# A gated attention and MLP kernel: four kinds of product share five PSUM banks in place of three and two

## The chip, the cores and the metric

The kernel runs on one core of one Trainium2 chip. The metric is device time in microseconds of one execution: the median of three runs before the change is 814.69 us (810.98 to 815.75).

## What is computed

The input x holds 2048 tokens of 512 numbers. Two branches read it: causal attention with 32 heads of 16 numbers and a sliding window of 256 tokens, and a two-layer MLP with 1792 hidden units and the tanh form of GELU. A gate, one number for each token, mixes them.

```python
def _A_ref(x, wqkv, wo):
    ...
    scores = jnp.einsum("bhqd,bhkd->bhqk", q, k) * (Dh ** -0.5)
    mask = (idx[:, None] - idx[None, :] >= 0) & (idx[:, None] - idx[None, :] < W)
    scores = jnp.where(mask[None, None], scores, -1e9)
    p = _softmax(scores, axis=-1)
    o = jnp.einsum("bhqk,bhkd->bhqd", p, v)
    return (lambda x, *d: x.transpose(*d))(o, 0, 2, 1, 3).reshape(B, S, D) @ wo

def _B_ref(x, w1, b1, w2, b2):
    h = _gelu(jnp.einsum("bsd,df->bsf", x, w1) + b1)
    return jnp.einsum("bsf,fd->bsd", h, w2) + b2

g = _sigmoid((x * gate_w).sum(-1, keepdims=True))
return g * a + (1 - g) * b
```

## The kernel before

The dense matrix products (the projections qk and v, the MLP's two layers u and y, the output projection a) are each made of three matmuls, since every operand is split into a high and a low part (`mm3`, lines 100 to 103). They work on tiles of 128 rows by 512 columns.

Attention takes four heads at a time: eight groups of heads, and in each 16 blocks of 128 tokens, so 128 steps of four heads. In each step and for each head three things happen.

- `att_max` (line 380) multiplies a block of 128 queries with up to 384 keys. This is the *maxima product*, the tile sm. VectorE adds a mask to it and takes each query's largest score (line 394, tile jm, the result in M).
- `att_exp` (line 424) multiplies a block of 128 keys with up to 384 queries, so that keys lie along the partitions. This is the *exponentials' product*, the tile st. ScalarE takes its exponential into pt (line 445), and GpSimd then zeroes what lies outside the window (lines 437 and 440).
- `att_pv` (line 451) multiplies those weights with the values (tile pv, line 465); ScalarE copies the finished sum out (line 476).

The maxima run six blocks ahead of the exponentials (LEAD). After each two blocks `att_rows` (line 400) negates the maxima on VectorE, and `att_turn` (line 409) turns them by a matmul with the identity: the *turned product*, tile mp. ScalarE writes it into 16 rows of the queries (line 418), so that the subtraction of the maximum is part of the exponentials' product. At the start of the kernel `qkv_x` (line 196) transposes blocks of x through TensorE: the *transposed product*, tile xp, which ScalarE and VectorE read.

The order of the instructions on TensorE, VectorE, ScalarE and GpSimd is written out by hand. The loop from line 708 issues for each head a maxima product, an exponentials' product, at one place the weighted sums and the turned product, and then as much dense work as the step's share of time (`fill`, 'mspf' in ORDER). Work of the other engines that follows from a product is put on a list with a due time by `after`, and `tick` advances a clock of planned times and issues what is due. Those planned times don't depend on PSUM. SP, which issues the DMAs, is left to a scheduler that orders by its own estimate of time. Each engine carries out its instructions in the order of its queue.

PSUM has eight banks, and each tile here takes one. Tiles with the same tag share as many banks as `bufs` says. A product whose bank still holds an unread one waits on TensorE, and all that follows it there waits too. Before, the banks were divided in this way: two for dense products (tag d), three for sm, mp and xp (tag sm), two for st (tag st), one for pv. Which of the banks of its tag a tile gets is settled when the program is built, from the same estimate of time that orders SP.

Of the kernel before, what the change touches and what calls it, by code (L numbers as in the profile page):

```python
# [9 lines left out]
F32 = mybir.dt.float32  # L10
# [11 lines left out]
NC = D // 128  # L22
# [10 lines left out]
def gated_mix(ctx: ExitStack, tc: tile.TileContext, x, wqkv, wo, w1, b1, w2, b2, gate_w, out):  # L33
# [7 lines left out]
    ps = ctx.enter_context(tc.tile_pool(name="ps", bufs=1, space=PSUM))  # L41
# [3 lines left out]
    def f32(ap):  # L45
        return ap.bitcast(F32)
# [61 lines left out]
    def after(ns, fn, *args):  # L108
        now[1] += 1
        heapq.heappush(todo, (now[0] + ns, now[1], fn, args))  # L110
# [7 lines left out]
    def tick(ns):  # L118
        now[0] += ns
        while todo and todo[0][0] <= now[0]:  # L120
            step_todo()

    def need(*keys):
        for key in keys:
            while key not in done:
                step_todo()
# [69 lines left out]
    def qkv_x(t, b):  # L196

        if b == 0:
            if t < NT - 1:
                v = (ks[:, 0], ks[:, 1], qs)[t].rearrange("p a c -> p (a c)")  # L200
                v = v.rearrange("p (c s t) -> p c s t", c=NC, s=2)
            else:
                v = sb.tile([128, NC, 2, T], F32R, tag="xt", bufs=1, name=f"xt{t}")
            xts[t] = v
        xt = xts[t]
        xr = xrs[t, b]
        p = ps.tile([128, NC, 128], F32, tag="sm", bufs=3, name=f"xp{t}_{b}")
        for c in range(NC):
            nc.tensor.transpose(p[:, c], xr[:, c * 128:(c + 1) * 128], ident)
        tick(4 * 110)  # L210

        def hi():
            nc.scalar.activation(xt[:, :, 0, b * 128:(b + 1) * 128], p, AF.Copy)

        def lo():
            nc.vector.tensor_sub(xt[:, :, 1, b * 128:(b + 1) * 128], p,
                                 f32(xt[:, :, 0, b * 128:(b + 1) * 128]))
            done.add(("x", t, b))
        after(100, hi), after(500, lo)
# [66 lines left out]
    def qkv(t):  # L286
# [4 lines left out]
        if t == 0:  # L291
            keys = qk + [("v", c) for c in range(NC)]
            load_xr(0)
            for key in keys[0:4]:
                load_raw(key, True)
            warm(WARM[0])
            for b in range(NB):
                qkv_x(0, b)
            warm(WARM[1])
            split(keys[0], nc.vector)  # L300
            split(keys[1], nc.vector)
            nc.sync.dma_start(gwb, gate_w.partition_broadcast(128))
        need(*[("x", t, b) for b in range(NB)])
        for n, (kind, j) in enumerate(pieces):
# [38 lines left out]
            if not last and n in xat:  # L343
                qkv_x(t + 1, xat.index(n))
# [35 lines left out]
    def att_max(g_, b, i):  # L380

        if b % RB == 0 and (g_, b // RB) not in Ms:
            Ms[g_, b // RB] = sb.tile([128, RB, 4], F32, tag="M", bufs=2, name=f"M{g_}_{b}")
        M = Ms[g_, b // RB]
        k0 = max(b - 2, 0) * 128
        w = (b + 1) * 128 - k0
        pr, s = divmod(i, 2)
        p = ps.tile([128, 384], F32, tag="sm", bufs=3, name=f"sm{g_}_{b}_{i}")
        nc.tensor.matmul(p[:, :w], qs[0:96, pr, b * 128:(b + 1) * 128], ks[0:96, pr, s, k0:k0 + w],  # L389
                         start=True, stop=True)  # L390
        junk = sb.tile([128, 384], BF16, tag="jm", bufs=1, name=f"jm{g_}_{b}_{i}")

        def red():
            nc.vector.tensor_tensor_reduce(junk[:, :w], p[:, :w], mask[:, 384 - w:384], 1.0, -3e38,  # L394
                                           ALU.add, ALU.max, M[:, b % RB, i:i + 1])
            done.add(("max", g_, b, i))
        tick(w / 2.4 + 13)
        after(100, red)
# [10 lines left out]
    def att_turn(g_, rb):  # L409

        need(("nm", g_, rb))
        p = ps.tile([112, 128], F32, tag="sm", bufs=3, name=f"mp{g_}_{rb}")
        nc.tensor.matmul(p, nms[rb % 2], identr, start=True, stop=True)  # L413

        def put():
            for b in range(RB):
                cols = slice((rb * RB + b) * 128, (rb * RB + b + 1) * 128)
                nc.scalar.activation(qs[96:112, :, cols], p[96:112].unsqueeze(1).broadcast_to([16, 2, 128]),  # L418
                    AF.Copy, scale=odd[96:112, b:b + 1])
            done.add(("rows", g_, rb))  # L420
        tick(67)
        after(100, put)

    def att_exp(g_, kb, i):

        pr, s = divmod(i, 2)
        w = min(384, S - kb * 128)
        if s == 0:
            pts[g_, kb, pr] = sb.tile([128, 2, 384], F32, tag="pt", bufs=11, name=f"pt{g_}_{kb}_{pr}")
        pt = pts[g_, kb, pr]  # L430
        need(*[("rows", g_, b) for b in range(kb // RB, (kb + w // 128 - 1) // RB + 1)])
        p = ps.tile([128, 384], F32, tag="st", bufs=2, name=f"st{g_}_{kb}_{i}")
        nc.tensor.matmul(p[:, :w], ks[:, pr, s, kb * 128:(kb + 1) * 128],  # L433
                         qs[:, pr, kb * 128:kb * 128 + w], start=True, stop=True)

        def sel():
            nc.gpsimd.affine_select(out=pt[:, :, 0:128], in_=pt[:, :, 0:128], pattern=[[0, 2], [1, 128]],  # L437
                                    compare_op=ALU.is_ge, fill=0.0, base=0, channel_multiplier=-1)
            if w == 384:
                nc.gpsimd.affine_select(out=pt[:, :, 256:384], in_=pt[:, :, 256:384], pattern=[[0, 2], [-1, 128]],  # L440
                                        compare_op=ALU.is_ge, fill=0.0, base=-1, channel_multiplier=1)
            done.add(("pt", g_, kb, pr))

        def exp():
            nc.scalar.activation(pt[:, s, :w], p[:, :w], AF.Exp, scale=SCALE)  # L445
            if s == 1:
                after(500, sel)
        tick(w / 2.4 + 13)
        after(100, exp)
# [258 lines left out]
    for u in range(-LEAD, NU):  # L708
        m = u + LEAD
        gm, bm = divmod(m, NKB)  # L710
        step = STEP if u >= 0 else STEP0
        for i in range(4):
            for op in ORDER:
                if op == "s" and u >= 0:
                    att_exp(u // NKB, u % NKB, i)
                if op == "m" and m < NU:
                    att_max(gm, bm, i ^ XOR)
                if op == "p" and i == PVAT and u >= 1:
                    att_pvs(u - 1)
                if op == "p" and i == PVAT and turn:  # L720
                    att_turn(*turn)
                    turn = None
                if op == "f":
                    fill(step / 4 / ORDER.count("f"))
        if m < NU and bm % RB == RB - 1:
            after(900, att_rows, gm, bm // RB)
            turn = (gm, bm // RB)
        if m % NB == LPOS and chunks:
            att_load(*chunks.pop(0))
        if u % NB == 2 and -NB < u < NU - NB:  # L730
            att_load_v(*divmod(u // NB + 1, NT))
# [47 lines left out]
```

## Time and profile before

| | |
|---|---|
| median of three runs | 814.69 us |
| the profiled execution, its own time | 813.36 us |
| span from its first to its last instruction | 811.4 us |
| stretch with attention steps of both kinds | about 157 to 760 us |
| granted TensorE clock | 1.000 |

The profile is of one execution. PE is TensorE's matmuls and PEld its weight loads, DVE is VectorE, ACT ScalarE, POOL GpSimd and SP the engine that issues DMAs; a trailing q (SPq) is the sequencer of an engine. A group's row gives the line, the engine, the operation, output<-input with shapes and the count; behind the first bar the busy time in us and the mean of one in ns; behind the second the idle time of the engine directly before these instructions, and what ended most of it. A row of the timeline gives start and duration in us, engine, line and operation, the count of merged instructions, and in brackets the idle time before it with what ended it. A row of a list of waits gives the sum in us, how many there were, and, where there is a third number, the longest. A view of one line lists what ended the idle time of its engine: us, then times.

### The profile page before, as it was taken

To read this page: it belongs to the slowest core of one execution; us is meant where nothing else is said; L and a number is where in the kernel's file an instruction comes from. 1 tells how busy PE (TensorE), PEld (TensorE's weight loads), DVE (VectorE), ACT (ScalarE), POOL (GpSimd) and SP (SyncE) were. 2 spreads that over 40 slices of the span, in tenths; PEclk is the share of its full clock that TensorE was granted. 3 is DMA by queue.
4 is the path that set the end of the run, shared out by engine and by line. 5 is a ranking of instruction groups with operands and counts; after the bars stand their busy time and mean duration, and the time that the engine had idled before them with its cause. 6 is when DMAs were issued, how large, how long until landed. Compare 5 with 4: busy or idle time off the path is not lost.

```text
span 811.4 us, 14841 instructions
## 1 busy us (share of the span) xinstructions
PE 788.5 (97%) x4694; PEld 616.6 (76%) x4694; DVE 513.7 (63%) x1517; ACT 483.4 (60%) x993; POOL 338.7 (42%) x611
## 2 busy tenths in 40 slices
PE   8999999999999999999999999999999999999998
PEld 6788888867877777688767867877777778777767
DVE  5433332887478758856885688568757865784353
ACT  4434423587568557755875677567656764876631
POOL 3200002396336425542784386336524552574100
PEclk9999999999999999999999999999999999999999
DMA  8985856536542734443234555542664363335873
GB/s 260 387 308 195 304 174 211 195 89 215 164 137 66 227 116 119 122 156 104 86 101 132 171 156 173 152 143 86 192 179 129 99 202 113 97 118 186 249 260 117
DMA packets 94925, 135.72 MB, mean 167 GB/s; under 512 B 32256, under 2 KB 43776, under 8 KB 94848
## 3 DMA queue, kind: packets, MB, share of 16 engines
q1 hardware_dynamic: 94848, 134.79, 52.3%
q8 instruction: 37, 0.61, 0.3%
q14 instruction: 40, 0.33, 0.1%
HBM read 79.70 MB, written 55.05 MB: 166 GB/s over the span
## 4 chain that ended last, share of the span: by engine, by line
PE 78%; DVE 8%; ACT 7%; DMA 2%; issue 2%; SPq 1%; POOL 1%; POOLq 0%; DVEq 0%; ACTq 0%
PE st L433 9%; PE pv L465 9%; PE sm L389 8%; PE y L101 6%; PE y L103 6%; PE y L102 6%; PE u L101 4%; PE u L102 4%; PE u L103 4%; PE qk L101 3%; PE qk L103 3%; PE qk L102 3%; DVE jm L394 2%; ACT pt L445 2%; PE v L103 2%
## 5 line engine op out<-in xcount | busy, mean ns | idle before, releaser
L394 DVE CUSTOM_DVE_ANT_0 jm<-sm,mask 128x384 bf16<-128x384 f32 (+2 forms) x512 | 270.6, 528 | 150.1 <-PE sm L389 128.7
L445 ACT ACTIVATE pt<-st 128x384 f32<-128x384 f32 (+2 forms) x512 | 231.0, 471 | 120.6 <-PE st L433 102.9
L437 POOL TENSOR_SCALAR_AFFINE_SELECT pt<-pt 128x256 f32<-128x256 f32 x256 | 122.3, 478 | 248.8 <-ACT pt L445 248.2
L433 PE MATMUL st<-qs,ks 128*128 128x384 f32 (+2 forms) x512 | 172.1, 338 | 8.1 <-ACT pt L445 7.1
L389 PE MATMUL sm<-ks,qs 96*128 96x384 f32 (+2 forms) x512 | 169.6, 332 | 1.8 <-DVE M L394 0.8
L433 PEld LDWEIGHTS st<-qs,ks 128*128 128x128 f32 x512 | 97.0, 190 | 37.1 <-ACT pt L445 19.4
L389 PEld LDWEIGHTS sm<-ks,qs 96*128 96x128 f32 x512 | 96.2, 188 | 26.0 <-DVE M L394 5.2
L440 POOL TENSOR_SCALAR_AFFINE_SELECT pt<-pt 128x256 f32<-128x256 f32 x224 | 101.9, 455 | 0.0
L465 PE MATMUL pv<-pt,vbuf 128*32 128x384 f32 (+2 forms) x1408 | 91.6, 389 | 0.1
L101 PE MATMUL y<-w,h 128*128 128x512 f32 x224 | 89.4, 399 | 0.0
L103 PE MATMUL y<-w,h 128*128 128x512 f32 x224 | 87.7, 391 | 1.3 <-POOL h L574 1.3
L102 PE MATMUL y<-w,h 128*128 128x512 f32 x224 | 87.7, 391 | 0.0
L574 POOL TENSOR_TENSOR h<-x1h,h 128x512 fp32r<-128x512 f32 x56 | 72.5, 1294 | 35.6 <-DVE h L571 35.2
L101 PE MATMUL u<-mx,w 128*128 128x512 f32 x196 | 79.3, 404 | 0.0
L102 PE MATMUL u<-mx,w 128*128 128x512 f32 x196 | 76.7, 391 | 0.0
L103 PE MATMUL u<-mx,w 128*128 128x512 f32 x196 | 76.6, 391 | 0.0
L418 ACT ACTIVATE qs<-mp,odd 16x256 fp32r<-16x256 f32 x128 | 53.0, 460 | 38.9 <-PE mp L413 37.9
L465 PEld LDWEIGHTS pv<-pt,vbuf 128*32 128x32 f32 x1408 | 38.5, 109 | 37.2 <-issue 24.2
L562 DVE SCALAR_TENSOR_TENSOR sqh<-sqh,x1h 128x512 f32<-128x512 f32 x56 | 51.6, 921 | 13.2 <-ACT sqh L559 13.2
L565 ACT ACTIVATE sqh<-sqh 128x512 f32<-128x512 f32 x56 | 35.5, 634 | 36.8 <-DVE sqh L562 36.2
L160 POOL TENSOR_TENSOR w<-raw_w,w 128x512 fp32r<-128x512 f32 x28 | 38.4, 1370 | 40.3 <-ACT w L156 40.2
L256 DVE TENSOR_TENSOR qke<-qk,qke 128x512 fp32r<-128x512 f32 x32 | 22.1, 691 | 51.3 <-ACT qke L253 49.6
(122 smaller groups left out, 1247.7 us busy)
## 6 DMA issues: line engine op xcount, KB each, us to landing
mx<-XT SPq DMA_DIRECT2D x24, 512.0 KB
SQ<-qke SPq DMA_DIRECT2D x16, 512.0 KB
SK<-qke SPq DMA_DIRECT2D x16, 512.0 KB
qs<-SQ SPq DMA_DIRECT2D x64, 128.0 KB
ND<-nd SPq DMA_DIRECT2D x32, 256.0 KB
ks<-SK SPq DMA_DIRECT2D x60, 128.0 KB
raw_w<-in_B_w_dram SPq DMA_DIRECT2D x28, 256.0 KB
SV<-vx SPq DMA_DIRECT2D x16, 272.0 KB
```

Source lines behind the costliest of these rows:

```text
L101: nc.tensor.matmul(p, lh, rh, start=first, stop=False)
L102: nc.tensor.matmul(p, lh, rl, start=False, stop=False)
L103: nc.tensor.matmul(p, ll, rh, start=False, stop=last)
L389: nc.tensor.matmul(p[:, :w], qs[0:96, pr, b * 128:(b + 1) * 128], ks[0:96, pr, s, k0:k0 + w], start=True, stop=True)
L394: nc.vector.tensor_tensor_reduce(junk[:, :w], p[:, :w], mask[:, 384 - w:384], 1.0, -3e38, ALU.add, ALU.max, M[:, b % RB, i:i + 1])
L418: nc.scalar.activation(qs[96:112, :, cols], p[96:112].unsqueeze(1).broadcast_to([16, 2, 128]), AF.Copy, scale=odd[96:112, b:b + 1])
L433: nc.tensor.matmul(p[:, :w], ks[:, pr, s, kb * 128:(kb + 1) * 128], qs[:, pr, kb * 128:kb * 128 + w], start=True, stop=True)
L437: nc.gpsimd.affine_select(out=pt[:, :, 0:128], in_=pt[:, :, 0:128], pattern=[[0, 2], [1, 128]], compare_op=ALU.is_ge, fill=0.0, base=0, ch ...
L440: nc.gpsimd.affine_select(out=pt[:, :, 256:384], in_=pt[:, :, 256:384], pattern=[[0, 2], [-1, 128]], compare_op=ALU.is_ge, fill=0.0, base= ...
L445: nc.scalar.activation(pt[:, s, :w], p[:, :w], AF.Exp, scale=SCALE)
L465: nc.tensor.matmul(pv[32 * i:32 * i + 32, q - c * T:e - c * T], vt[:, 68 * (kb % NB) + 17 * i:68 * (kb % NB) + 17 * i + 32], pts[g_, kb, i ...
L574: nc.gpsimd.tensor_sub(h[:, 1], x1, f32(h[:, 0]))
```

## The change

The four tags of attention's and the transposes' products become one tag with five banks. The instructions and their order in the source stay; the count of banks stays eight.

```diff
 def qkv_x(t, b):
-        p = ps.tile([128, NC, 128], F32, tag="sm", bufs=3, name=f"xp{t}_{b}")
+        p = ps.tile([128, NC, 128], F32, tag="s", bufs=5, name=f"xp{t}_{b}")
 ...
 def att_max(g_, b, i):
-        p = ps.tile([128, 384], F32, tag="sm", bufs=3, name=f"sm{g_}_{b}_{i}")
+        p = ps.tile([128, 384], F32, tag="s", bufs=5, name=f"sm{g_}_{b}_{i}")
 ...
 def att_turn(g_, rb):
-        p = ps.tile([112, 128], F32, tag="sm", bufs=3, name=f"mp{g_}_{rb}")
+        p = ps.tile([112, 128], F32, tag="s", bufs=5, name=f"mp{g_}_{rb}")
 ...
 def att_exp(g_, kb, i):
-        p = ps.tile([128, 384], F32, tag="st", bufs=2, name=f"st{g_}_{kb}_{i}")
+        p = ps.tile([128, 384], F32, tag="s", bufs=5, name=f"st{g_}_{kb}_{i}")
```

## The prediction

> **What bounds the kernel now.** The page comes first: its busy shares, its chain and its costliest groups.
>
> ```profile
> span 811.4 us, 14841 instructions
> ...
> PE 788.5 (97%) x4694; PEld 616.6 (76%) x4694; DVE 513.7 (63%) x1517; ACT 483.4 (60%) x993; POOL 338.7 (42%) x611
> ...
> PE 78%; DVE 8%; ACT 7%; DMA 2%; issue 2%; SPq 1%; POOL 1%; POOLq 0%; DVEq 0%; ACTq 0%
> ...
> L394 DVE CUSTOM_DVE_ANT_0 jm<-sm,mask 128x384 bf16<-128x384 f32 (+2 forms) x512 | 270.6, 528 | 150.1 <-PE sm L389 128.7
> L445 ACT ACTIVATE pt<-st 128x384 f32<-128x384 f32 (+2 forms) x512 | 231.0, 471 | 120.6 <-PE st L433 102.9
> ```
>
> TensorE is the bound: 97% busy, 78% of the chain. The engines that empty the four kinds of product are free a third of the time: VectorE waits 128.7 us for maxima products (sm) and ScalarE 102.9 us for exponential products (st). So this change can win only what TensorE loses to a bank that is not yet empty. The views of the lines L433 and L389 tell what ended TensorE's idle time before them (matmuls and weight loads added together), and here are their complete lists, with the one that counts stand-alone waits:
>
> ```profile
>   ACT pt L445: 26.5, 54
> ...
>   DVE M L394: 6.0, 16
>   ACT qs L418: 3.5, 7
> ...
> L389 PEldq EVENT_SEMAPHORE  x165: 51/51/51, 129.4 to 732.5; - x165
> ```
>
> No DMA is in these lists. Together 36.0 us, but a stalled product shows its gap twice, under its matmul and under its weight load. What it truly costs is read from start to start, in the timeline:
>
> ```profile
> 161.78 0.44 PE L389 MATMUL sm<-ks,qs 96*128 96x384 f32 x1 [0.44 <-DVE M L394]
> ...
> 398.89 0.55 DVE L394 CUSTOM_DVE_ANT_0 jm<-sm,mask 128x384 bf16<-128x384 f32 x1
> ...
> 399.29 0.33 PE L433 MATMUL st<-qs,ks 128*128 128x384 f32 x1
> ...
> 399.59 0.56 DVE L394 CUSTOM_DVE_ANT_0 jm<-sm,mask 128x384 bf16<-128x384 f32 x1
> ...
> 399.79 0.34 PE L433 MATMUL st<-qs,ks 128*128 128x384 f32 x1
> ...
> 400.30 0.56 DVE L394 CUSTOM_DVE_ANT_0 jm<-sm,mask 128x384 bf16<-128x384 f32 x1
> ...
> 400.65 0.34 PE L389 MATMUL sm<-ks,qs 96*128 96x384 f32 x1
> ...
> 400.92 0.87 ACT L445 ACTIVATE pt<-st 128x384 f32<-128x384 f32 x2
> ...
> 401.46 0.19 PEld L433 LDWEIGHTS st<-qs,ks 128*128 128x128 f32 x1 [0.85 <-ACT pt L445]
> 401.46 0.44 PE L433 MATMUL st<-qs,ks 128*128 128x384 f32 x1 [0.48 <-ACT pt L445]
> ...
> 402.44 0.34 PE L389 MATMUL sm<-ks,qs 96*128 96x384 f32 x1
> ...
> 402.61 0.34 PE L433 MATMUL st<-qs,ks 128*128 128x384 f32 x1
> ...
> 403.47 0.34 PE L389 MATMUL sm<-ks,qs 96*128 96x384 f32 x1
> ...
> 403.94 0.19 PEld L433 LDWEIGHTS st<-qs,ks 128*128 128x128 f32 x1 [0.51 <-ACT pt L445]
> ...
> 404.42 0.49 ACT L445 ACTIVATE pt<-st 128x384 f32<-128x384 f32 x1 [0.15 <-PE st L433]
> ...
> 717.99 0.44 PE L433 MATMUL st<-qs,ks 128*128 128x384 f32 x1 [0.40 <-ACT pt L445]
> ```
>
> Unhindered, st starts 0.17 us after its sm (402.44, 402.61). At 401.46 it started 0.81 us after it, so 0.64 us are lost, where the view shows 0.48 + 0.85. At 403.94 it lost 0.47 - 0.17 = 0.30 us, where it shows 0.51. Per microsecond shown that is 0.94 / 1.84 = 0.51, and 36.0 x 0.51 = 18.4 us. Taking the same difference for every sm, st and turned (mp) product that started within 0.12 us of the emptying of its bank, I find 48 waits, from one before the sm at 161.78 to one before the st at 717.99, and 17.4 us in all: 13.5 at 33 st, 3.9 at 15 sm, none at mp. **17.4 us is all that banks cost now**, 2.1% of the time.
>
> **The change, part by part.**
>
> *Order.* Within TensorE, VectorE, ScalarE and GpSimd no instruction moves; counts and durations stay. Moved are waits, which follow from what the bank of a product held before, and some DMA issues on SP. The built program fixes the bank of each product. It doesn't count the five banks round, but hands out whichever bank its planner thinks free first. For the 48 waits of today it gives:
>
> ```
> bank's last product: before -> after          waits   us now   us left
> st: st two back      -> an sm                   22      9.1      2.2
> st: st two back      -> an mp or older st        3      1.9      0
> st: st two back      -> the same st              8      2.5      2.5
> sm: sm               -> an st or older sm        5      1.3      0
> sm: sm or mp         -> one emptied as late     11      2.6      2.5
> ```
>
> "Left" is the same subtraction again, with the end of the emptying that the changed bank waits for, everything else at its time of today. Example: the st at 401.46 gets the bank of the sm whose maxima ran from 400.30 to 400.86, so nothing holds it at 400.65 + 0.17. **Relieved: 17.4 - 7.2 = 10.2 us.**
>
> *New waits.* By the same subtraction 17 products that start freely today find their new bank still full: 4.9 us in all. Five (1.2 us) are st behind late maxima or a late turned product: the st of 399.29 gets a bank whose maxima ran from 398.89 to 399.44, and the st at 399.79 one whose maxima end at 400.15, so TensorE gives up 0.36 + 0.05 = 0.41 us by there. In seven (1.7 us) an sm gets the bank of the st *directly before it*; in five (2.0 us) the product two before. The dearest:
>
> ```profile
> 613.49 0.34 PE L433 MATMUL st<-qs,ks 128*128 128x384 f32 x1
> ...
> 613.67 0.34 PE L389 MATMUL sm<-ks,qs 96*128 96x384 f32 x1
> ...
> 613.93 0.88 ACT L445 ACTIVATE pt<-st 128x384 f32<-128x384 f32 x2 [0.88 <-PE st L433]
> ```
>
> One exponential of this shape takes 0.49 us (404.42), so the first of the pair that starts at 613.93 ends at 614.42. From an emptying to its waiter it is 0.05 us (the pair of 400.92: 401.41, and st at 401.46). So the sm of 613.67 starts at 614.47, 0.80 us later. Behind it in TensorE's queue stand the next st, three dense matmuls and the weighted sums (pv); VectorE and ScalarE wait for those.
>
> *What the rest costs.* TensorE gets 39 more stand-alone waits: 39 x 51 ns = 2.0 us at worst; I take 0, since the 165 of today's sm products end none of the idle time in their list. The turned products wait behind other banks in 27 of 64 cases, but follow the weighted sums, which cover it; I take 0, at worst 0.8 us each. The transposes of x go from three banks to five; they wait for DMA alone:
>
> ```profile
> L209 PE MATMUL xp<-identr,xr 128*128 128x128 f32 x64 | 9.9, 280 | 2.4 <-DMA xr<-in_A_x_dram 2.4
> ...
> SPq L477 <- ACT nd L476: 96.8, 29, 9.9
> ...
> 206.66 0.30 SPq L354 DMA_DIRECT2D qs<-SQ  x1
> ...
> 223.43 0.34 PE L389 MATMUL sm<-ks,qs 96*128 96x384 f32 x1
> ```
>
> On SP, stores of weighted sums (L477) move past loads of keys (L353, L354) by a few places, a load of wo by a dozen. Such a store holds the queue up to 9.9 us. The loads behind it have a lead: one of the shortest runs from 206.66 to the first sm that needs its chunk at 223.43, 16.8 us, and no DMA ends a wait of L389. I take 0; without that cover one late chunk would cost up to 9.9 us.
>
> *Sum at rest:* -10.2 + 4.9 = -5.3 us. But an emptying that is late because its engine is busy doesn't come earlier when TensorE does. The cluster above, worked through: 0.94 relieved, 0.41 new, so TensorE is 0.5 us ahead at 403.94. Then:
>
> ```profile
> 406.72 1.33 DVE L562 SCALAR_TENSOR_TENSOR sqh<-sqh,x1h 128x512 f32<-128x512 f32 x1
> ...
> 407.97 0.55 DVE L394 CUSTOM_DVE_ANT_0 jm<-sm,mask 128x384 bf16<-128x384 f32 x1
> ...
> 408.58 0.19 PEld L389 LDWEIGHTS sm<-ks,qs 96*128 96x128 f32 x1 [0.31 <-DVE M L394]
> ...
> 409.54 0.44 PE L433 MATMUL st<-qs,ks 128*128 128x384 f32 x1 [0.52 <-ACT pt L445]
> ```
>
> The sm at 408.58 keeps its bank, whose maxima stand at 407.97 behind a GELU step of 1.33 us, and that step waits for ScalarE, which from 404.42 on had no idle time to give up but the 0.15 us before that row. So the lead shrinks from 0.5 to some 0.15 us, until the st at 409.54 gives its wait back. Between all kept and all lost (-5.3 and 0) I take half: **-2.7 us.** 813.36 - 2.7 = 810.7 on the profiled execution. That execution lies 1.3 us below the median of the runs shown, so the prediction is 814.69 - 2.7 = **812.0 us**.
>
> [...]
>
> **Rivals.**
>
> *More is kept.* Every relief holds and the new waits vanish into idle time elsewhere: 814.69 - 10.2 = 804.5 us. For it: ScalarE and VectorE have 103 and 129 us of waiting for TensorE. Against: today's waits stand in clusters where just those engines are late. If the banks were simply enough, all 17.4 us would go: 797.3 us; the eight and eleven waits whose bank is as late as now exclude that. [...]
>
> *Slower.* The mechanism is the near neighbour: 13 sm or mp products take the bank of a product one or two before, where today the nearest is three back. If each costs what the one at 613.67 does, 13 x 0.80 = 10.4 us, and the relief is wholly met again, the time is 825.1 us. It decides from about 8.1 us on, that is ten of the 13 at full price. Against: seven of them cost 1.7 us together at today's times, because ScalarE is mostly past them. With the 4.9 us of today's times and no relief: 819.6 us.
>
> *It does nothing.* The five banks were eight minus three before, and TensorE issues in order: a late emptier stops it either way, one product later. Then 814.7 us, -1 to +2.
>
> **How the numbers follow.** Forecast (809.5 to 813.7) 0.45; nothing (to 816.7) 0.23; more is kept 0.14; slower 0.18. A change of 1%, 8.1 us, is about what a measurement of this kernel can tell from none. Faster by over 1% is the half of "more is kept" near its end, 0.07; slower by over 1% the two thirds of "slower" near its own, 0.13; the rest 0.80. The range goes from full relief, 804.5, to all new waits without relief, 819.6, rounded to 805 and 820; beyond lie some 0.17.
>
> **What would show it.** Right: in the view of L433 the idle time ended by ACT falls from 26.5 to under 15 us and VectorE appears there, which it doesn't now; in that of L389 the list gains "ACT pt". Idle time at both together falls from 36.0 to some 30. Near neighbours: sm waits of 0.5 to 0.8 us directly behind an st. Wrong, if ACT's share at L433 stays, if L389's idle time passes 20 us, or if a DMA ends waits there.

## The result: 0.4% slower

| | before | changed |
|---|---|---|
| median of 19 runs | 813.34 us | 817.40 us |
| range | 810.98 to 817.73 | 813.90 to 819.51 |
| the profiled execution, its own time | 813.36 us | 814.35 us |
| its span and granted clock | 811.4 us, 1.000 | 812.6 us, 0.997 |

The ratio is 1.0041, 95% interval 1.0030 to 1.0051: within 1%, and clearly on the other side of no change than forecast. That is 3.3 us (0.41% of 813.34); the two medians lie 4.1 us apart. From the page of the changed kernel, the rows that answer to those of before, and behind them the lists of what ended TensorE's idle time at L433 and at L389:

```profile
span 812.6 us, 14882 instructions
...
PE 791.9 (97%) x4694; PEld 617.7 (76%) x4694; DVE 514.7 (63%) x1517; ACT 482.8 (59%) x993; POOL 339.1 (42%) x611
...
L433 PE MATMUL st<-qs,ks 128*128 128x384 f32 (+2 forms) x512 | 172.4, 339 | 5.1 <-DVE M L394 2.2
L389 PE MATMUL sm<-ks,qs 96*128 96x384 f32 (+2 forms) x512 | 170.8, 335 | 3.4 <-DVE M L394 1.1
```

```profile
  ACT pt L445: 9.6, 26
  DVE M L394: 9.1, 19
  ACT qs L418: 0.4, 1
...
  ACT pt L445: 5.8, 14
  DVE M L394: 5.0, 11
  ACT qs L418: 4.5, 10
```

The change did what it says: exponentials' products now wait less for ScalarE (26.5 us before, 9.6 now) and also for VectorE, and maxima products wait for ScalarE's exponentials. But the sum fell from 36.0 to 34.4 us only. Counted from start to start, as in the prediction, the products lose 16.6 us to full banks, against 17.4 before. The waits have moved rather than gone.

Two places show where time went. The first is the near neighbour that the prediction priced, now in the changed kernel's own timeline:

```profile
614.08 0.33 PE L433 MATMUL st<-qs,ks 128*128 128x384 f32 x1
...
614.51 0.49 ACT L445 ACTIVATE pt<-st 128x384 f32<-128x384 f32 x1 [0.88 <-PE st L433]
...
615.05 0.44 PE L389 MATMUL sm<-ks,qs 96*128 96x384 f32 x1 [0.64 <-ACT pt L445]
```

The sm starts 0.97 us behind its st where 0.18 would do: 0.79 us lost, for 0.80 forecast. ScalarE had been idle for 0.88 us before that exponential, so it could not have come sooner. It is the only one of this size: the seven sm that get the bank of the st directly before them lose 1.2 us together in this trace. Four st that get the bank of the product two before lose 1.9 us.

The second place lies behind the products. At this point of the dense work TensorE needs the low half of a hidden tile, which GpSimd makes at the end of a chain over VectorE and ScalarE (L562 to L574). First the row of before, then two of the changed kernel:

```profile
426.49 0.50 PE L103 MATMUL y<-w,h 128*128 128x512 f32 x1 [1.35 <-POOL h L574]
```

```profile
422.50 0.39 PE L102 MATMUL y<-w,h 128*128 128x512 f32 x1
425.02 0.50 PE L103 MATMUL y<-w,h 128*128 128x512 f32 x1 [2.13 <-POOL h L574]
```

```profile
426.00:428.00 2.00, 2.00 (x19) 1.31 (x12) 0.31 (x2) 1.14 (x3) 0.00 (x0) 0.50 0.00 0
428.00:430.00 2.00, 2.00 (x8) 1.67 (x8) 1.39 (x4) 1.22 (x4) 0.67 (x2) 0.65 0.34 131
```

The first two fences are the timeline of TensorE; the third is the table of stretches, with busy time of PE, PEld, DVE, ACT and POOL, then the granted TensorE clock, DMA share and GB/s. Before, the same wait was 1.35 us. In this execution TensorE came there 2.25 us earlier (the matmul ahead of the wait ends at 422.89, before at 425.14). Of that, 1.5 us come from the start of the kernel, where the first blocks of x landed sooner this time; the tile's chain has them too. The other 0.8 us were won in attention, and were waited off. Just behind that, the clock is 0.50 for 2 us and 0.65 for the next 2: together about 3.4 us at half speed (2.0 + 0.35 x 2 / 0.5), which costs TensorE some 1.7 us. In the profile of before the clock is 1.000 here.

TensorE carries out the same matmuls in the same order in both kernels, so the two traces can be laid side by side, start against start. The changed execution wins 0.75 us between 160 and 424 us, gives up 0.8 at this wait and 1.5 in the slow stretch behind it, and loses another 1.1 us by the end: 2.7 us in all. Because of the earlier blocks of x the two executions' own times differ by only 1.0 us.

How often the clock falls below 1.000 differs too. With the run's mean granted clock beside each run, 17 of 19 runs of the changed kernel are below 1.000. Of the runs of the kernel before in the three sets of experiments, each on a chip of its own, it was 10 of 35, 9 of 23 and 1 of 25. Where in a run the clock fell is known for the profiled executions alone. In the first of these sets the median of the runs of before is 813.0 us at 1.000 (25 runs) and 815.8 us at 0.998 (8 runs). The two runs of the changed kernel at 1.000 have a median of 814.7 us, and its ten at 0.998 one of 817.9 us.

So two theories stood. **Theory 1:** the banks are about even, and the loss comes behind them, in the lead that is waited off at 425 us and the half clock that follows. **Theory 2:** the new waits made by the choice of banks are the loss.

### The profile page after: what moved, and what is told of

Its sections match the earlier page's. It is cut to its first block, busy times and chain, and to the rows that moved or that the text cites. A ratio compares the mean times of both kernels' runs of the same rounds, so it can differ in the third digit from the quotient of the medians.

```text
span 812.6 us, 14882 instructions
## 1 busy us (share of the span) xinstructions
PE 791.9 (97%) x4694; PEld 617.7 (76%) x4694; DVE 514.7 (63%) x1517; ACT 482.8 (59%) x993; POOL 339.1 (42%) x611
## 4 chain that ended last, share of the span: by engine, by line
PE 79%; DVE 9%; ACT 6%; issue 3%; DMA 2%; POOL 0%; SPq 0%; DVEq 0%; ACTq 0%; POOLq 0%
PE st L433 9%; PE pv L465 9%; PE sm L389 8%; PE y L101 6%; PE y L103 6%; PE y L102 6%; PE u L101 4%; PE u L102 4%; PE u L103 4%; PE qk L103 4%; PE qk L101 4%; PE qk L102 4%; DVE jm L394 3%; DVE sqh L562 2%; ACT pt L445 2%
## 5 line engine op out<-in xcount | busy, mean ns | idle before, releaser
L445 ACT ACTIVATE pt<-st 128x384 f32<-128x384 f32 (+2 forms) x512 | 230.2, 471 | 121.1 <-PE st L433 102.7
L433 PE MATMUL st<-qs,ks 128*128 128x384 f32 (+2 forms) x512 | 172.4, 339 | 5.1 <-DVE M L394 2.2
L389 PE MATMUL sm<-ks,qs 96*128 96x384 f32 (+2 forms) x512 | 170.8, 335 | 3.4 <-DVE M L394 1.1
L433 PEld LDWEIGHTS st<-qs,ks 128*128 128x128 f32 x512 | 97.2, 190 | 33.3 <-ACT pt L445 8.1
L389 PEld LDWEIGHTS sm<-ks,qs 96*128 96x128 f32 x512 | 96.5, 188 | 30.1 <-ACT pt L445 4.8
L103 PE MATMUL y<-w,h 128*128 128x512 f32 x224 | 87.8, 392 | 2.1 <-POOL h L574 2.1
L574 POOL TENSOR_TENSOR h<-x1h,h 128x512 fp32r<-128x512 f32 x56 | 72.5, 1294 | 37.5 <-DVE h L571 36.8
L103 PE MATMUL u<-mx,w 128*128 128x512 f32 x196 | 76.6, 391 | 0.0
L562 DVE SCALAR_TENSOR_TENSOR sqh<-sqh,x1h 128x512 f32<-128x512 f32 x56 | 52.1, 930 | 13.2 <-ACT sqh L559 13.2
```

Of the source, the lines that this page charges most:

```text
L103: nc.tensor.matmul(p, ll, rh, start=False, stop=last)
L562: nc.vector.scalar_tensor_tensor(sq, sq, GC, x1, op0=ALU.add, op1=ALU.mult)
L574: nc.gpsimd.tensor_sub(h[:, 1], x1, f32(h[:, 0]))
```

## The experiments

### The hidden tile out of the way, in both kernels

In both kernels the low half of that one hidden tile is made on VectorE, directly behind its cast, in place of GpSimd. Everything else stands as it was.

```diff
         def f5():
             nc.vector.tensor_copy(h[:, 0], x1)
+            f6() if h.name[:4] == "h2_6" else None
         def f6():
-            nc.gpsimd.tensor_sub(h[:, 1], x1, f32(h[:, 0]))
+            if h.name not in done: (nc.vector if h.name[:4] == "h2_6" else nc.gpsimd).tensor_sub(h[:, 1], x1, f32(h[:, 0]))
             done.add(h.name)
```

> The kernel before, with one subtraction moved: the low half of the hidden tile for which TensorE waits at 426.49 (1.35 us idle, ended by POOL h L574) is made on VectorE directly behind its cast, not on GpSimd. Both theories: that idle time goes, nothing else moves much, -1.3 us, ratio 0.9984 (0.997 to 1.000). Granted clock 1.000 as in the profile of before.

> The changed kernel with the same subtraction moved. Theory 1 (the banks themselves are about even, and the loss comes behind them: the lead is waited off at the hidden tile, 2.13 us idle, and in 3.4 us at half clock behind it): no clock below 1.000 near 425 us, and a time equal to that of the kernel before with the same move, to within 1 us, ratio to before 0.997 to 1.000. Theory 2 (the new waits that the planner's choice of banks makes are the loss): the change still costs some 3 us over the kernel before with this move, ratio 1.001 to 1.004.

> before_hv once more, on the same chip as its neighbours: 812 to 813 us, some 1 us below the kernel before.

> after_hv once more, on the same chip as its neighbours: 814 to 815 us, 1.5 to 2.6 us above before_hv2.

Measured against the kernel before: before_hv 813.14 us, ratio 0.9996 (0.9977 to 1.0015); after_hv 814.75 us, 1.0012 (0.9998 to 1.0025). On a second chip: before_hv2 811.51 us, 0.9981 (0.9971 to 0.9991); after_hv2 813.23 us, 1.0010 (0.9999 to 1.0022). Both lie some 0.5 to 1 us below what was expected there, and their difference where it was expected.

Both theories hold a part. With the tile moved the change costs 1.6 and 1.7 us by the medians (814.75 - 813.14, 813.23 - 811.51), in place of some 3.3 us (0.41%). The runs at a clock of 1.000 alone give 2.6 us (814.7 against 812.1) and 0.9 us (812.8 against 811.9), so this cost is known to about 1 us. Moving the tile wins 0.29 to 0.31% in the changed kernel (from 1.0041 to 1.0012 and 1.0010) and 0.04 to 0.19% in the kernel before. The changed kernel's clock follows: it was 1.000 in 9 of 12 runs of after_hv and in 10 of 12 of after_hv2, where the change alone had 2 of 19. The clock of the kernel before doesn't: 7 of 12 runs of before_hv and 9 of 12 of before_hv2 are at 1.000, where 25 of 35 and 24 of 25 of the kernel before on the same chips are. The expectation had 1.000.

What is left isn't all due to the banks. In after_hv TensorE still waits for this tile, now for VectorE, where in before_hv it doesn't:

```profile
426.33 0.50 PE L103 MATMUL y<-w,h 128*128 128x512 f32 x1 [0.71 <-DVE h L574]
```

Side by side with before_hv2, from the beginning of attention on, after_hv2 loses 2.5 us in the profiled executions: the st win 2.0 and the sm lose 2.4, the turned products lose 0.7, the matmul at this tile 0.75, and the others together 0.7.

### The near neighbours taken out of the change

The bank of each product is written into the program as a list: five tags of one bank, and a digit for each product. The list is the changed kernel's own, except where a product would get the bank of one or two products back; there it takes the oldest one, 24 times.

```diff
+    turns = iter(BANKS)
...
-        p = ps.tile([128, 384], F32, tag="s", bufs=5, name=f"sm{g_}_{b}_{i}")
+        p = ps.tile([128, 384], F32, tag=f"r{next(turns)}", bufs=1, name=f"sm{g_}_{b}_{i}")
 ...
```

The tiles xp, mp and st get their tags in the same way.

> The changed kernel's own banks, except that the 24 products which get the bank of one or two products back take the oldest bank instead (the two banks change their parts from there on); with the tile of 426 us out of the way. By subtraction in the trace of before 7.2 us are left, as in the change, and the new waits fall from 4.9 to 1.2 us. If near neighbours are what the change loses, the time falls by 3 us or more against after_hv2, to before_hv2 or below. If they are cheap, it falls by less than 1 us.

Measured: 809.78 us, ratio 0.9974 (0.9960 to 0.9988), beside after_hv2's 813.23 us on the same chip. That is 3.45 us less by the medians and 2.9 by the two ratios (0.0036 of 812.74), of 3.7 expected at rest (4.9 - 1.2). The place shown above runs through:

```profile
611.11 0.34 PE L433 MATMUL st<-qs,ks 128*128 128x384 f32 x1
611.28 0.34 PE L389 MATMUL sm<-ks,qs 96*128 96x384 f32 x1
611.46 0.34 PE L433 MATMUL st<-qs,ks 128*128 128x384 f32 x1
```

Idle time before sm ended by "ACT pt L445" falls with it; in the lists of L389 of after_hv2 and of after_far_hv:

```profile
  ACT pt L445: 6.1, 15
  DVE M L394: 5.1, 11
  ACT qs L418: 5.1, 10
```

```profile
  DVE M L394: 5.7, 13
  ACT qs L418: 4.6, 10
  ACT pt L445: 2.7, 8
```

At st the same line falls from 10.1 to 6.5 us. Of the 24 products 11 are st that had the bank of the product two before, a distance that 21 st of the kernel before have too; 13 are sm or mp. Side by side, TensorE wins 2.4 us at st and 1.0 at sm, so the st are the larger part.

This settles theory 2 for the banks' part: the near neighbours are what sharing five banks loses here. Without them the kernel is not slower than before_hv2. By the medians it is 1.7 us faster (811.51 - 809.78), by the ratios 0.6 (0.9981 and 0.9974), and the intervals of these overlap, so a win is not shown by this run alone.

### Other ways to hand out the same five banks

Three lists of digits: strict turn (`next(turns) % 5`), the order in which the trace of before shows the banks emptied, and that order taken again from the trace of the kernel so made. The first two were run with the hidden tile as it was and with it moved, the third only with it moved.

> Five banks in strict turn, so that no product gets the bank of one less than five back. Theory 2 (near neighbours are the loss): the waits of sm directly behind st go, and the time falls to that of before or below, ratio 0.997 to 1.000. Theory 1: near neighbours were cheap (1.1 us in the profile after), strict turn makes as many other waits (subtracting in the trace of before: 8.2 us left and 7.5 us new, against 7.2 and 4.9 for the change), and the time stays with the changed kernel's or above it, ratio 1.002 to 1.008.

> Strict turn, with the same tile out of the way. Both differ from after_hv (814.7 us, clock 1.000 in 9 of 12 runs) only in the choice of banks. If near neighbours and unlucky choices of the planner are what after_hv loses against before_hv (812.1 us at clock 1.000), then 812 to 813.5 us; if any sharing of five banks costs that, 814 to 816 us.

> The same five banks, but each product gets the bank that the trace of before shows emptied first. The subtraction gives 6.0 us left and no new wait, so -11.3 us at rest. Theory 2: most of it is kept, ratio 0.988 to 0.995. Theory 1: the banks' waits fall, but lateness of VectorE and ScalarE is met elsewhere (other banks, hidden tiles, weighted sums), so at most 3 us are kept, ratio 0.996 to 1.003, and the idle time ended by POOL or by POOL's hidden tiles grows.

> Banks by the order in which the trace of before shows them emptied, and the low half of the hidden tile of 426 us on VectorE. Theory 1 (what the shared banks win is waited off at that tile, with 3.4 us or more at half clock behind it): with the tile out of the way the win stays, and the clock is 1.000 in most runs, 808 to 810 us, ratio 0.993 to 0.996. If the win was waited off elsewhere too: as before_hv, 0.9975 to 1.000.

> As measured_hv, with the banks in the order in which the trace of measured_hv itself shows them emptied (48 of 1104 products change their bank's last user). If the order of emptying is what decides, 807.5 to 809.5 us, at or a little below measured_hv; if it was luck of one trace, 811 us or more.

| | median | ratio to before |
|---|---|---|
| ring | 815.99 us | 1.0022 (1.0005 to 1.0039) |
| ring_hv | 814.31 us | 1.0012 (0.9995 to 1.0030) |
| measured | 811.81 us | 0.9974 (0.9960 to 0.9989) |
| measured_hv | 809.21 us | 0.9935 (0.9915 to 0.9955) |
| measured2_hv | 806.97 us | 0.9931 (0.9920 to 0.9943) |

ring and measured, with the tile as it was, came out in the ranges of theory 1.

Strict turn has no near neighbour, and yet is no better than before. Its waits are of another kind: in ring_hv the list of L433 holds a single line, 31.6 of the 40.6 us in the lists of L433 and L389.

```profile
  DVE M L394: 31.6, 57
```

With sm and st in alternation, the product five back is mostly one of the other kind: 367 of the 512 st get the bank of an sm, against 275 in the change. So more st hang on maxima, and VectorE is the engine that is late in lumps (the GELU step of 1.33 us in the prediction). ring_hv met the expectation that any sharing costs (814 to 816 us), while after_far_hv refutes that reading: the choice costs, not the sharing. That strict turn was dear for this reason is read from its list, not separated by a run of its own.

The order of emptying wins. measured_hv keeps 0.65% (6 runs) and measured2_hv 0.69% (5 runs), and measured2_hv is the fastest of all kernels here: 806.97 us, half a microsecond below what was expected. Some of that is the moved tile, which alone wins 0.04 to 0.19%. Without the tile's move most of the win is lost: measured has the wait at 424.6 us, 2.07 us idle in its timeline, and below-1.000 clock in 10 of 12 runs, and keeps 0.26%.

```profile
424.61 0.80 PE L103 MATMUL y<-w,h 128*128 128x512 f32 x1 [2.07 <-POOL h L574]
```

Up to there it was 1.4 us further ahead than at the beginning of attention (starts of the same matmul in both traces: -1.13 us at 160 us, -2.50 at 420); at 440 it was 1.1 us behind before. Of these 3.6 us, 0.7 are the longer wait; the rest goes with 6.8 us at half clock behind it (424.49 to 431.31 us; the mean granted clock of this execution is 0.996, of the one before 1.000). That is theory 1, shown on a kernel whose banks do win.

### Does the longer wait halve the clock?

In the kernel before, GpSimd makes that low half twice.

```diff
-            nc.gpsimd.tensor_sub(h[:, 1], x1, f32(h[:, 0]))
+            for _ in range(2 if h.name[:4] == "h2_6" else 1): nc.gpsimd.tensor_sub(h[:, 1], x1, f32(h[:, 0]))
```

> The kernel before, with that hidden tile's subtraction on GpSimd done twice, so that TensorE waits some 1.3 us longer at 426 us (2.6 us in place of 1.35 idle). If a wait of over 2 us is what halves the clock for 3.4 us, the clock is below 1.000 in nearly all runs and the time is 1.3 + 1.7 = 3.0 us or more above before, ratio 1.003 to 1.006. If the drop has another cause, the clock stays at 1.000 in most runs as before, and the time is 1.3 us up or less, ratio 1.000 to 1.002.

Measured: 815.81 us, ratio 1.0023 (1.0004 to 1.0042). 8 of 12 runs are below 1.000, where 9 of 23 of the kernel before on that chip are. This lies between the two expectations. The profiled execution waited even longer than any other, and kept its clock:

```profile
428.49 0.50 PE L103 MATMUL y<-w,h 128*128 128x512 f32 x1 [2.74 <-POOL h L574]
```

```profile
428.00:430.00 2.00, 1.51 (x19) 0.91 (x19) 0.57 (x2) 0.49 (x1) 1.15 (x3) 1.00 0.43 112
```

So a wait of over 2 us doesn't decide the drop. That it makes one more likely is suggested by 8 of 12 against 9 of 23, not shown. What decides it is not shown either: the clock fell at waits of 2.13 us in the changed kernel, 2.07 us in measured and 2.15 us in ring (there for the first blocks of x), and around the 2.74 us here it is 1.00 in each of the three stretches of 2 us from 426 to 432 us.

### Nothing shared: three banks for st, two for sm, mp and xp

Against the kernel before; mp and xp change as sm does, and the hidden tile is moved as above.

```diff
-        p = ps.tile([128, 384], F32, tag="sm", bufs=3, name=f"sm{g_}_{b}_{i}")
+        p = ps.tile([128, 384], F32, tag="sm", bufs=2, name=f"sm{g_}_{b}_{i}")
...
-        p = ps.tile([128, 384], F32, tag="st", bufs=2, name=f"st{g_}_{kb}_{i}")
+        p = ps.tile([128, 384], F32, tag="st", bufs=3, name=f"st{g_}_{kb}_{i}")
```

> Nothing shared: three banks for the exponentials' products and two for the others, with the same tile out of the way. Tells which side is short. By subtraction in the trace of before: of 17.4 us 11.8 are left, and 41 us of new waits arise at 96 products, nearly all sm behind maxima that are not yet taken. So 820 to 850 us, and the idle time before sm, ended by VectorE, over 20 us. If VectorE's side had banks to spare, 808 to 812 us.

Measured in two runs: 824.72 us, ratio 1.0132 (1.0097 to 1.0167). Idle time at st is gone, its list is empty; at sm it is

```profile
  DVE M L394: 40.8, 74
  ACT qs L418: 17.1, 22
```

So VectorE's side needs its three banks. The total is 12 to 13 us above before_hv and before_hv2; the subtraction at rest would have given 41 - 5.6 = 35 us. So here new waits, nearly all behind a late VectorE, count for less than half of their length, even if all the relief was kept (17 to 19 of 41 us).

## Why the prediction was wrong

*What bounds the kernel* was right: TensorE, and 17.4 us at full banks. So was the reading of what the change moves: the signs at L433 and L389 came, except the fall of their sum to 30 us (34.4), and of sm waits of 0.5 to 0.8 us behind an st there is one. Its table adds up to 49 waits, one sm more than the 48 of its text; the sums in us agree. SP's new order and the extra stand-alone waits cost nothing that shows: no DMA ends a wait in the lists, and the kernels with the measured order have as many extra waits (44) and are the fastest. The turned products, taken at nothing too, lose 0.7 us start to start. The base was high as well: 814.69 us is the median of three runs, 813.34 that of 19. From the latter the same forecast would be 810.6 us, and further off.

*The step that failed is the sum at rest and its halving.* The prediction set 10.2 us of relief against 4.9 us of new waits, and took half of the difference. The runs show that these two don't shrink alike (us, by the medians and, in brackets, by the ratios):

| | at rest | in the runs |
|---|---|---|
| near neighbours: after_hv2 against after_far_hv | +3.7 | +3.45 (+2.9) |
| relief less the other new waits: after_far_hv against before_hv2 | -10.2 + 1.2 = -9.0 | -1.7 (-0.6) |
| measured order, second pass: measured2_hv against before_hv2 | -11.3, from the first pass | -4.5 (-4.1) |
| nothing shared: st3sm2_hv against before_hv and before_hv2 | 41 - 5.6 = +35 | +12 to 13 |

The new waits at near neighbours count for four fifths or more. The engine that the dearest of them waits for was idle until the product came (0.88 us before the exponential of 614.51). Relief counts for at most a fifth in one choice of banks and some two fifths in another. The new waits behind a late VectorE count for less than half. That the difference lies in whether the awaited engine is idle or late fits all four rows; no run changes that alone. Where relief goes can be seen side by side: from before_hv2 to after_far_hv the st win 4.4 us, and the sm lose 1.4 of it again, the matmul at the hidden tile 0.7 and the turned products 0.6. The example that the prediction itself worked through kept 0.15 of 0.5 us, which is nearer to that than the half it took.

*The step that was missing* is the place of 426 us. The prediction asked what the products would meet next among the banks, and didn't look for other waits of TensorE further on. The page of before had it, among the rows of L103, as 1.3 us ended by "POOL h L574". The lead of 0.8 us won ahead of it was worth nothing here, and cost more: in the profiled execution a wait 0.8 us longer, and 1.5 us lost at half clock behind it. That most of the runs at a clock below 1.000 lost it at this place is likely, since moving the tile mostly ends it (9 and 10 of 12 runs at 1.000, in place of 2 of 19), but only profiled executions show the place. In that of ring the clock fell behind the first blocks of x (0.67, 0.50 and 0.98 in the stretches of 2 us from 28 to 34 us). That of measured_hv has a mean clock of 0.998, and no sm or st matmul in it ran longer than 446 ns, where the longest of the changed kernel took 629, so there too it likely fell outside attention. With the tile moved, the change costs some 1.7 us, 0.75 of them still at that tile in the profiled execution; with the tile as it was, some 3.3 us.

*The rival "slower"* had the right mechanism: near neighbours. Its size was some 3 us for the 24 products one or two back, not 10.4 us for 13, and the larger part fell on the 11 st that this rival had not counted. That the one at 613.67 was the dearest of them was said in the prediction; to price all by it was only a bound. *"More is kept"* fell, as far as the change goes. What it names was there to be had, though: with the banks in the order of emptying and the tile out of the way the kernel wins 0.69%. *"It does nothing"* comes nearest for the products themselves: in after_hv2 the st win 2.0 us and the sm lose 2.4, so a late emptier mostly stops TensorE at another product.

*Still open:* which of strict turn's waits are its loss, what decides whether the clock falls at a wait, why it stayed down for 6.8 us in measured and 3.4 us in the changed kernel, and how large the banks' own part is to better than 1 us.

## What to carry to other kernels

Price a wait that a change adds near its full length where the awaited engine stands idle until the product comes (here 2.9 to 3.45 of 3.7 us), and a wait behind a late engine, added or taken away, at a fraction (here 12 to 13 of 35 us added, and 0.6 to 4.5 of some 9 to 11 us taken away). Equal terms of both signs need not cancel. What a pool that shares banks was worth here hung on the order in which it handed them out: the same five banks gave ratios from 0.9931 to 1.0012 with the tile out of the way. So look at what each product's bank held last, and keep a bank from going back to a product one or two places on (24 such products cost some 3 us here). Before counting a lead of the bounding engine as won, list that engine's other waits further on: here a wait that was 0.8 us longer than before took back the 0.8 us won up to 425 us.

## What was not expected of the hardware

- About 3.4 us at half TensorE clock, in the middle of a kernel whose TensorE is 97% busy, behind a single wait of 2.1 us, while a wait of 2.74 us in before_late had none. A drop shows in the profile of ring too, where the first x blocks came late: 2.15 us idle, then a clock of 0.67, 0.50 and 0.98 in three stretches of 2 us.

```profile
28.31 0.82 PE L209 MATMUL xp<-identr,xr 128*128 128x128 f32 x4 [2.15 <-DMA xr<-in_A_x_dram]
```

```profile
28.00:30.00 2.00, 1.69 (x7) 1.50 (x8) 0.33 (x2) 0.83 (x2) 0.00 (x0) 0.67 1.08 404
30.00:32.00 2.00, 2.00 (x6) 1.52 (x6) 0.49 (x1) 0.80 (x2) 1.12 (x1) 0.50 1.02 398
32.00:34.00 2.00, 2.00 (x10) 1.65 (x9) 0.00 (x0) 0.59 (x2) 0.15 (x1) 0.98 1.02 416
```

- Single runs of the kernel before at a mean clock of 0.998 lie 2.8 us above those at 1.000 (815.8 and 813.0 us). A drop as in the profile of the changed kernel, 3.4 us at half clock, would account for some 1.7 us of it; the rest is not shown. This is more than the banks' own part, so that the clock beside each run has to be read before a difference of this size.
